# The second channel weight rounded beside the attention and kept in DRAM, and three of the four first token products made of seven smaller products

## The chip, the core and the metric

The program runs on one core of one Trainium2 chip. The core has five engines that run their own instruction streams in order: TensorE (PE in the profile; its weight loads are PEld), VectorE (DVE), ScalarE (ACT), GpSimd (POOL) and SyncE (SP), which here only issues transfers. They hand work to each other by semaphores. The metric is the device time of one execution in microseconds (us); the kernel before has a median of 803.48 us over 5 runs, from 801.98 to 804.40.

## The reference

```python
# attention, 4 batches x 8 heads, S = 768, D = 64; 6 hash bits for each query and key
mask   = q_bucket[:, :, :, None] == k_bucket[:, :, None, :]
scores = scale * np.matmul(q, k.transpose(0, 1, 3, 2))
scores = np.where(mask, scores, -1000000000.0)
attn   = softmax(scores);  x = np.matmul(attn, v)          # (B, S, H*D) = (4, 768, 512)
# mixer: tokens, then channels
h  = np.maximum(x.transpose(0, 2, 1) @ w_tok1, 0.0) @ w_tok2   # 768 -> 256 -> 768
u  = x + h.transpose(0, 2, 1)
h2 = np.maximum(u @ w_ch1, 0.0) @ w_ch2                        # 512 -> 1536 -> 512
out = u + h2
```

The four weights arrive as 64-bit floats. The kernel turns each into 32-bit floats itself ("rounding" below).

## The kernel before

The kernel has three stages after each other, every one with its own pools and with its instructions in the order in which the source writes them: `attention`, `tokens`, `channels`. A fourth part behind a branch is taken only for inputs of large size and does not run here.

**Attention** loops over 16 pairs of heads (n = 0 to 15, four pairs for a batch), and each pair has two halves of 384 queries. For a half, `scores` makes six score tiles: two 32-bit products of keys and queries (L337, `sc<-qk`), then two short bf16 products with the hash bits (L337, `sc<-bits`), which push scores of unequal buckets far down. ScalarE makes the exponential of each tile (L344, `e`), VectorE adds the six tiles up (`add` and `add_last`: L371, L375, L378, tile `esd`), and `weigh` multiplies with the values (L389, `acc`). Three score tiles fit in PSUM; the hash product and one `acc` take their turns in the same ring of three.

The hash bits of pair n+1 are made in pair n by `hashes`: a product (L298, `hp`), VectorE's sign test (L302, `g`), ScalarE's scaling (L303), and eight small transfers by SyncE into the tile `bits` (L308). Transfer 0 to 3 hold what the first half's queries and the first three key blocks need, transfers 6 and 7 the last three key blocks. In the order of pair n's instructions `hashes(n + 1)` stands after the adds of both halves but the last one, then come `add_last`, `load_qk(n + 2)`, `add_values` (L289), rounding, and the normalisation of pair n-1 (`newton` L426 and L428, copies L434, `divide` L438). Behind every second pair, `bounce` transposes two pairs into DRAM (L233, L238), from where `fetch` reads a batch back in token order (L245).

Rounding is the class `Conversion`. A block is 128 x 768 numbers: `fetch` loads its raw words (L169, 768 KB), `begin` is one ScalarE instruction (L177), `join` four VectorE instructions (L187, L191, L195, L196), and `end` one more (L206) that writes the rounded block. `one()` is begin, join, end and the next fetch; `turnover()` is end and fetch. In the attention the blocks of `w_tok1`, `w_tok2` and `w_ch1` (12 in all) are rounded, one in each of pairs 0 to 11, with two buffers of raw words and one fetch ahead. The eight blocks of `w_ch2` are rounded in the stage `tokens`, one by one as "jobs" between its products, straight into the tile `WC2`.

**Tokens** loops over the four batches. `mix1(b)` is the first token product: 12 products with 512 columns (L634), each shown as two rows because a 32-bit product takes two passes; ScalarE applies relu (L641). `mix2(b, m)` is the second token product, already written as seven products in place of eight (L674) with ScalarE copies (L679 to L686), VectorE adds (L689 to L693) and `left_sums` (L657 to L660); its result goes by an accumulating transfer from GpSimd (L694) into `XT`. The results are collected in three `places`, so the transfer of a place has to land before the place is written again. The order is mix1(0), mix1(1), mix2(0,0), mix2(0,1), mix1(2), and so on; at the end come mix2(3,0), mix2(3,1). Both token stages use eight PSUM banks in turn. `weight_sums` of the first channel weight (L724 to L729) is the first job.

**Channels** (L761 and the rows around it) follows with products of the same seven-for-eight kind. Its last one writes four quarters of the output, each with a transfer of its own: L1173, L1180 and twice L1185, issued by ScalarE in the very last product and by SyncE in the one before.

```python
            weights.begin()
            if before:
                before.newton()
            weights.join()
            halves[0].weigh()
            ...
            if before:
                before.divide()
            weights.turnover()
            halves[1].weigh()
```

Of the kernel before, what the change touches and what calls it, by code (L numbers as in the profile page):

```python
# [34 lines left out]
F32 = mybir.dt.float32  # L37
BF16 = mybir.dt.bfloat16
U32 = mybir.dt.uint32
# [9 lines left out]
def kernel(  # L49
# [13 lines left out]
    nc = tc.nc  # L63
# [77 lines left out]
    class Conversion:  # L141


        def __init__(self, pool, parts, bufs):
            self.pool, self.bufs = pool, bufs
            self.todo = [
                (w, dst, rows, j, n)
                for w, dst, rows, blocks in parts
                for j in range(*blocks, rows)
                for n in range(0, dst.shape[2], NW // rows)  # L150
            ]
            self.fetched, self.begun, self.ready = [], None, None
            for _ in range(bufs - 1):
                self.fetch()
# [25 lines left out]
        def join(self):  # L180
            if not self.begun:
                return
            raw, size, to, rows = self.begun
            self.begun = None
            unit = self.pool.tile([P, NW], F32, name="unit", tag="unit", bufs=1)

            nc.vector.tensor_scalar(  # L187
                unit.bitcast(U32), size.bitcast(U32), 3, 0x7F800000,
                op0=ALU.logical_shift_left, op1=ALU.bitwise_and,
            )  # L190
            nc.vector.tensor_scalar(  # L191
                size.bitcast(U32), size.bitcast(U32), 3, None, op0=ALU.logical_shift_left,
            )

            nc.vector.scalar_tensor_tensor(unit, raw[:, :, 0], 2.0**-52, unit, op0=ALU.mult, op1=ALU.mult)  # L195
            nc.vector.tensor_tensor(size, size, unit, op=ALU.add)  # L196
            self.ready = raw, size, to, rows

        def end(self):

            if not self.ready:
                return
            raw, size, to, rows = self.ready
            self.ready = None
            hi, size = (a.rearrange("p (t n) -> p t n", t=rows) for a in (raw[:, :, 1], size.bitcast(U32)))
            nc.vector.scalar_tensor_tensor(  # L206
                to.bitcast(U32), hi, 0x80000000, size, op0=ALU.bitwise_and, op1=ALU.bitwise_or,
            )

        def turnover(self):  # L210
# [13 lines left out]

    dram = ctx.enter_context(tc.tile_pool(name="dram", bufs=1, space=bass.MemoryType.DRAM))
    bounced = [dram.tile([S, DM], F32, name=f"bounced{b}") for b in range(B)]

# [30 lines left out]
    def attention(pool, psum, W1, W2, x0):  # L258
# [191 lines left out]
        for _ in range(12):  # L450
# [3 lines left out]
            pool,  # L454
            [(w_tok1, W1, 3, (0, NR)), (w_tok2, W2, 1, (0, NJ)), (w_ch1, WC1, 1, (0, NCB))],
            bufs=2,
# [4 lines left out]
        for n in range(len(pairs)):  # L461
# [3 lines left out]
            for now in halves:  # L465
                now.scores()
                if n == now.half == 0:
                    hashes(1)
                now.add()
                if now.half == 0:  # L470
                    now.add_last()
            if before:
                before.sums()
# [20 lines left out]
            if before:  # L494
                before.divide()
            weights.turnover()
            halves[1].weigh()
            if n and n % 2 == 0:
# [93 lines left out]

    def tokens(pool, psum, W1, W2, x0, weights, jobs, T, places):

# [5 lines left out]
        R1 = {}  # L600
        turned = not jobs
        if not turned:
            fetch(1, x1)
            jobs = jobs(weights(pool))
            bounce(places[2], len(pairs) - 2)
        NQ = DM // 2
        sums = pool.tile([P, 3, HALF], F32, name="W2sums", tag="W2sums", bufs=1)
        b00, b01, b10, b11 = (W2[:, k, HALF * n : HALF * n + HALF] for k in range(2) for n in range(2))

        def weight_sums():  # L610
            nc.vector.tensor_tensor(sums[:, 0], b01, b00, op=ALU.subtract)
            nc.vector.tensor_tensor(sums[:, 1], b11, sums[:, 0], op=ALU.subtract)
            nc.vector.tensor_tensor(b01, b11, b01, op=ALU.subtract)
            nc.vector.tensor_tensor(sums[:, 2], b10, sums[:, 1], op=ALU.subtract)

        def job():
            if not turned and jobs:
                jobs.pop(0)()

# [3 lines left out]
        def banks():  # L623
            return psum.tile([P, 2, 512], F32, name="trp", tag="tr", bufs=2)

        def mix1(b):
            x = (x0, x1)[b % 2]
            if b and turned:
                turn(b, x, banks)
            r1 = pool.tile([P, NJ, DM], F32, name="r1", tag="r1", bufs=2)  # L630
            for j in range(NJ):
                ps = bank("t1")
                for r in range(NR):
                    nc.tensor.matmul(  # L634
                        ps, W1[:, r, P * j : P * j + P], x[:, r], start=(r == 0), stop=(r == NR - 1),
                    )
                to = r1[:, j]
                if not turned:
                    to = to.rearrange("p (c g i) -> p g c i", c=NCB, i=32)
                    ps = ps.rearrange("p (g c i) -> p g c i", c=NCB, i=32)  # L640
                nc.scalar.activation(to, ps, ACT.Relu)  # L641
                job()
            if b % 2:
# [3 lines left out]
            R1[b] = r1, new  # L647
            if not turned and b + 2 < B:
                fetch(b + 2, x)

# [11 lines left out]
        def mix2(b, m):  # L662
# [5 lines left out]
            new = new[:, :, P * m : P * m + P]  # L668
            ps = [bank("t2")[:, :HALF] for _ in range(4)]
            to = places[(2 * b + m + 1) % 3].rearrange("p (i n t) -> p i n t", i=2, n=2)  # L670
            p1, u, p7, p57 = (to[:, i, n] for i in range(2) for n in range(2))

            def product(at, left, right, start=True):
                nc.tensor.matmul(  # L674
                    ps[at], left, right, start=start, stop=True, skip_group_check=True,
                )

            product(0, a00, b00)
            nc.scalar.copy(p1, ps[0])  # L679
            product(1, a01, b10)  # L680
            product(2, s1, sums[:, 0])
            nc.scalar.copy(p57, ps[2])
            product(3, new[:, 1], b01)
            nc.scalar.copy(p7, ps[3])
            product(0, new[:, 0], sums[:, 1], False)
            nc.scalar.copy(u, ps[0])  # L686
            product(2, new[:, 2], b11, False)
            product(3, a11, sums[:, 2], False)
            nc.vector.tensor_tensor(p1, ps[1], p1, op=ALU.add)  # L689
            nc.vector.tensor_tensor(p57, p7, p57, op=ALU.add)  # L690
            nc.vector.tensor_tensor(p57, p57, u, op=ALU.add)  # L691
            nc.vector.tensor_tensor(p7, ps[3], u, op=ALU.add)
            nc.vector.tensor_tensor(u, ps[2], u, op=ALU.add)  # L693
            nc.gpsimd.dma_start(  # L694
                out=XT[:, 2 * m : 2 * m + 2, S * b : S * b + S], in_=to.rearrange("p i n t -> p i (n t)"),
                accum_op=ALU.add,
            )

        for b in range(B):
            mix1(b)  # L700
            if b == 0:
                weight_sums()
            left_sums(b)
            if b:
                mix2(b - 1, 0)
                job()
                mix2(b - 1, 1)
        mix2(B - 1, 0)
        inputs(0, T, 0)
        mix2(B - 1, 1)  # L710
        while not turned and jobs:
            job()

# [19 lines left out]
    def channels(pool, psum, SW1, second, TA, judge):  # L733
# [399 lines left out]
        def product(s, j, name, q, between, final=None):  # L1133
# [38 lines left out]
            if final:  # L1172
                issuer.dma_start(out=final(0, 0), in_=qs[:, 0])  # L1173
            nc.vector.tensor_tensor(p57[:, 0], p57[:, 0], p57[:, 1], op=ALU.add)
            if j < 6 and final:
                begin(ORDER[j + 1])
            if final:
                nc.vector.tensor_tensor(qs[:, 3], qs[:, 3], u, op=ALU.add)
                nc.vector.tensor_tensor(qs[:, 3], qs[:, 3], p57[:, 0], op=ALU.add)
                issuer.dma_start(out=final(1, 1), in_=qs[:, 3])  # L1180
                for i in (1, 2):
# [177 lines left out]
    def attention_and_tokens(W1, W2, x0):  # L1359
# [12 lines left out]

        def weights(pool):
            return Conversion(pool, [(w_ch2, WC2, 3, (0, NHT))], bufs=3)

        def jobs(conversion):
            early, late = weight_sums(
                WC1, SW1, slice(0, NCB // 2), slice(NCB // 2, NCB), slice(0, DCH // 2), slice(DCH // 2, DCH),
            )
            return [  # L1380
                lambda: (early(), late()),
                *[conversion.one] * (NHT * DM // NW),
            ]

        SW2 = second["SW2"].rearrange("p i k c -> p i (k c)")
        places = [SW2[:, i] for i in range(3)]
        inside(tokens, W1, W2, x0, weights, jobs, [TA[:, 0], None, TA[:, 1], None], places)

    def careful_attention_and_tokens(W1, W2, x0):
# [11 lines left out]
        TA = big["TA"]  # L1401
        with tc.tile_pool(name="places", bufs=1, reuse_waits="tile") as pool:
            places = [pool.tile([P, 2 * S], F32, name=f"place{i}") for i in range(3)]
            inside(tokens, W1, W2, x0, None, None, [TA[:, 0], None, TA[:, 1], None], places)

# [49 lines left out]
```

## Time and profile before

| | |
|---|---|
| median of 5 runs | 803.48 us (801.98 to 804.40) |
| the profiled execution: its own time | 804.27 us |
| the profiled execution: its span | 802.5 us |
| PE busy | 792.8 us, 99% of the span |
| DVE busy | 657.8 us, 82% |
| ACT busy | 441.5 us, 55% |
| attention, from the first product to the first L634 | up to 315.5 us of the span |
| tokens, L634 to the first L761 | 315.5 to 394.0 us |
| channels, L761 | 394.0 to 794.8 us, then the last adds and transfers |

Times in the text are microseconds from the start of the span. A row of the timeline has a start, a length, the engine, the source line, the operation, the tiles (written <- read), the shape and a count of merged instructions; in brackets stands the idle time of that engine just before, with what ended it. A "q" after an engine's name means its sequencer, as when it issues a transfer. The span is 1.77 us shorter than that execution's own time, and that execution is 0.79 us above the median of the runs.

### The profile page before, as it was taken

To read this page: it belongs to the slowest core of one execution; us is meant where nothing else is said; L and a number is where in the kernel's file an instruction comes from. 1 tells how busy PE (TensorE), PEld (TensorE's weight loads), DVE (VectorE), ACT (ScalarE), POOL (GpSimd) and SP (SyncE) were. 2 spreads that over 40 slices of the span, in tenths; PEclk is the share of its full clock that TensorE was granted. 3 is DMA by queue.
4 is the path that set the end of the run, shared out by engine and by line. 5 is a ranking of instruction groups with operands and counts; after the bars stand their busy time and mean duration, and the time that the engine had idled before them with its cause. 6 is when DMAs were issued, how large, how long until landed. Compare 5 with 4: busy or idle time off the path is not lost.

```text
span 802.5 us, 10594 instructions
## 1 busy us (share of the span) xinstructions
PE 792.8 (99%) x3885; PEld 470.7 (59%) x3885; DVE 657.8 (82%) x881; ACT 441.5 (55%) x707; POOL 53.7 (7%) x77
## 2 busy tenths in 40 slices
PE   9999999999999999999999999999999999999996
PEld 5444444444444444455444458876667886666885
DVE  4889898989887677999677888988769897679985
ACT  5688888888888886333222221327782335774110
POOL 1000000000000000011121010011110012100010
PEclk9999999999999999999999999999999999999998
DMA  4435353537352424797636994599754577630455
GB/s 163 159 121 160 121 160 121 161 121 239 126 168 91 148 71 158 199 292 176 155 68 207 312 378 165 179 292 287 212 150 147 208 200 198 208 105 15 175 179 113
DMA packets 90972, 138.61 MB, mean 173 GB/s; under 512 B 29656, under 2 KB 63392, under 8 KB 88608
## 3 DMA queue, kind: packets, MB, share of 16 engines
q1 hardware_dynamic: 82192, 112.20, 42.1%
q0 software_dynamic: 7728, 24.64, 13.7%
q10 hardware_dynamic: 992, 1.00, 0.4%
q8 instruction: 33, 0.54, 0.3%
q14 instruction: 27, 0.22, 0.1%
HBM read 97.21 MB, written 33.16 MB: 162 GB/s over the span
## 4 chain that ended last, share of the span: by engine, by line
PE 95%; DVE 2%; DMA 1%; issue 0%; ACT 0%; DVEq 0%; ACTq 0%
PE b L761 50%; PE sc L337 20%; PE acc L389 16%; PE t L634 4%; PE t L674 2%; PE sums L413 2%; PE hp L298 1%; DMA XT<-second 1%; PE hw L316 1%; PE idle L451 0%; DVE size L196 0%; DVE unit L195 0%; DVE second L693 0%; DVE second L691 0%; DVE second L689 0%
## 5 line engine op out<-in xcount | busy, mean ns | idle before, releaser
L344 ACT ACTIVATE e<-sc 128x768 f32<-128x768 f32 x192 | 154.0, 811 | 12.7 <-PE sc L337 12.3
L337 PE MATMUL sc<-qk 64*128 64x384 f32 x768 | 156.7, 487 | 0.0
L761 PE MATMUL b<-R,second 128*128 128x256 f32 (+1 forms) x612 | 150.9, 404 | 0.0
L761 PEld LDWEIGHTS b<-R,second 128*128 128x128 f32 x612 | 116.3, 190 | 31.6 <-issue 17.2
L767 ACT COPY c<-b 128x512 f32<-128x512 f32 (+1 forms) x78 | 37.5, 488 | 169.1 <-PE b L761 158.5
L389 PE MATMUL acc<-e,vn 128*64 128x384 f32 x768 | 127.6, 488 | 0.0
L375 DVE TENSOR_TENSOR esd<-esd,e 128x768 f32<-128x768 f32 x96 | 92.0, 958 | 10.0
L389 PEld LDWEIGHTS acc<-e,vn 128*64 128x64 f32 x768 | 53.6, 137 | 73.1 <-issue 71.1
L337 PEld LDWEIGHTS sc<-qk 64*128 64x128 f32 x768 | 67.5, 187 | 49.1 <-issue 47.6
L761 PE MATMUL b<-XT,WC 128*128 128x256 f32 (+1 forms) x264 | 82.5, 456 | 0.0
L761 PEld LDWEIGHTS b<-XT,WC 128*128 128x128 f32 x264 | 50.2, 190 | 29.6 <-issue 24.9
L337 PE MATMUL sc<-bits 64*128 64x384 bf16 x384 | 62.9, 323 | 0.2 <-DVE bits L320 0.2
L371 DVE SCALAR_TENSOR_TENSOR esd<-e 128x768 f32<-128x768 f32 x32 | 30.6, 955 | 28.1 <-ACT e L344 28.1
L634 PE MATMUL t<-x,W 128*128 128x512 f32 x96 | 41.8, 593 | 0.0
L694 POOL DMA_DIRECT2D XT<-second x8 | 9.9, 1232 | 392.1 <-DVE second L693 366.1
L395 ACT ACTIVATE num<-acc,vsum 128x384 f32<-128x384 f32 x32 | 18.6, 581 | 31.8 <-PE acc L389 31.4
L434 ACT COPY rec<-rec 32x384 f32<-32x384 f32 x64 | 32.6, 509 | 5.0 <-DVE rec L428 4.2
L761 PE MATMUL b<-XT,SW 128*128 128x256 f32 (+1 forms) x120 | 34.6, 422 | 0.0
L337 PEld LDWEIGHTS <-bits 64*128 64x128 bf16 x384 | 19.3, 94 | 25.4 <-DVE bits L320 0.8
L761 PE MATMUL b<-TA,WC 128*128 128x512 f32 x72 | 33.8, 592 | 0.0
L761 PE MATMUL b<-TA,SW 128*128 128x512 f32 x72 | 32.9, 592 | 0.0
L378 DVE TENSOR_TENSOR esd<-esd,e 128x768 f32<-128x768 f32 x32 | 30.5, 954 | 1.9
(214 smaller groups left out, 1131.1 us busy)
## 6 DMA issues: line engine op xcount, KB each, us to landing
second<-left SPq DMA_DIRECT2D x18, 1344.0 KB
raw<-in_moe_w_ch SPq DMA_DIRECT2D x16, 768.0 KB
qk<-in_qk SPq DMA_DIRECT2D x15, 768.0 KB
seen<-in_qk POOLq DMA_DIRECT2D x21, 384.0 KB, 3.9
WC<-hidden_left SPq DMA_DIRECT2D x15, 448.0 KB
vn<-in_v SPq DMA_DIRECT2D x16, 384.0 KB
vt<-in_vT SPq DMA_DIRECT2D x16, 384.0 KB
x<-bounced SPq DMA_DIRECT2D x4, 1536.0 KB
```

What stands on the lines that cost most here:

```text
L337: nc.tensor.matmul(sc[:, i, :HALF], t[rows, 1, P * c : P * c + P], t[rows, 0, qs], start=start, stop=not start,)
L344: nc.scalar.activation(e, sc[:, :, :HALF], ACT.Exp, scale=SCALE)
L371: nc.vector.scalar_tensor_tensor(self.d, es[0], NR * EPS, es[1], op0=ALU.add, op1=ALU.add,)
L375: nc.vector.tensor_tensor(self.d, self.d, e, op=ALU.add)
L378: nc.vector.tensor_tensor(self.d, self.d, self.es[-1], op=ALU.add)
L389: nc.tensor.matmul(acc[D * i : D * i + D], vn[:, i, c], e[:, i], start=(c == 0), stop=(c == NR - 1),)
L395: nc.scalar.activation(nums[self.n][:, self.half], acc, ACT.Identity, scale=-1.0, bias=vsum,)
L413: nc.tensor.matmul(ps[at : at + 32], ones[:, :32], self.halves[h].d[:, i], start=True, stop=True,)
L434: nc.scalar.copy(rec[other : other + 32, h], rec[at : at + 32, h])
L634: nc.tensor.matmul(ps, W1[:, r, P * j : P * j + P], x[:, r], start=(r == 0), stop=(r == NR - 1),)
L761: nc.tensor.matmul(ps, left(k), right(k), start=start and k == ks[0], stop=stop and k == ks[-1], skip_group_check=True,)
L767: nc.scalar.copy(c, ps)
```

## The change

1. The eight blocks of `w_ch2` join the list that the attention rounds, so there are 20 blocks for 16 pairs. One block is rounded in each pair as before, now in all 16, and in pairs 1, 5, 9 and 13 a second one by `weights.one()`, between the adds of the first half and those of the second half. One more fetch at the end of pair 0 puts the raw words two blocks ahead. A rounded block of `w_ch2` is written to the tile `unit` and from there by a SyncE transfer to a DRAM tile `wc2`; after mix1(0) one transfer brings all 3 MB of it into `WC2`. The conversions in `tokens` are gone.
2. mix1(1), mix1(2) and mix1(3) are made of seven products each, three instructions of 256 columns to a product, with sums of `W1` made once (`left`, four VectorE instructions), sums of x for every such batch (`right_sums`, four), four ScalarE copies and five VectorE adds (`seven`, which mix2 now shares), and two relus afterwards (`relus`). mix1(0) keeps its full product, in 24 instructions of 256 columns in place of 12 of 512. The two halves of the sums of the first channel weight are jobs after batches 0 and 1.
3. In the last channel product the first two of the four output transfers are issued by SyncE, the last two by ScalarE as before.

```diff
             away = to.space == bass.MemoryType.DRAM
             nc.vector.scalar_tensor_tensor(
-                to.bitcast(U32), hi, 0x80000000, size, op0=ALU.bitwise_and, op1=ALU.bitwise_or,
+                (unit if away else to).bitcast(U32), hi, 0x80000000, size,
+                op0=ALU.bitwise_and, op1=ALU.bitwise_or,
             )
+            if away:
+                nc.sync.dma_start(out=to, in_=unit)
...
-            [(w_tok1, W1, 3, (0, NR)), (w_tok2, W2, 1, (0, NJ)), (w_ch1, WC1, 1, (0, NCB))],
+            [
+                (w_tok1, W1, 3, (0, NR)), (w_tok2, W2, 1, (0, NJ)), (w_ch1, WC1, 1, (0, NCB)),
+                (w_ch2, wc2, 3, (0, NHT)),
+            ],
             bufs=2,
...
                 now.add()
                 if now.half == 0:
                     now.add_last()
+                    if n % 4 == 1:
+                        weights.one()
...
             weights.turnover()
+            if n == 0:
+                weights.fetch()
             halves[1].weigh()
...
+        def right_sums(b):
+            x00, x01, x10, x11 = quarters(b)
+            nc.vector.tensor_tensor(right[:, 0], x01, x00, op=ALU.subtract)
+            nc.vector.tensor_tensor(right[:, 1], x11, right[:, 0], op=ALU.subtract)
+            nc.vector.tensor_tensor(x01, x11, x01, op=ALU.subtract)
+            nc.vector.tensor_tensor(right[:, 2], x10, right[:, 1], op=ALU.subtract)
...
+            seven([bank("t1")[:, :NQ] for _ in range(4)], to, [
+                (u00, x00), (u01, x10), (s1, t1), (s3, x01), (s2, t2), (s4, x11), (u11, t4),
+            ])
...
+        weight_sums()
+        if not turned:
+            bounce(places[2], len(pairs) - 2)
+            right_sums(1)
         for b in range(B):
+            if b and turned:
+                turn(b, (x0, x1)[b % 2], banks)
+                right_sums(b)
             mix1(b)
-            if b == 0:
-                weight_sums()
+            if not turned:
+                if b + 2 < B:
+                    fetch(b + 2, (x0, x1)[b % 2])
+                if b == 0:
+                    nc.sync.dma_start(out=second["WC2"], in_=wc2)
+                elif b + 1 < B:
+                    right_sums(b + 1)
+            if b:
+                mix2(b - 1, 0)
+                relus(b)
             left_sums(b)
             if b:
-                mix2(b - 1, 0)
-                job()
                 mix2(b - 1, 1)
+            if jobs:
+                jobs.pop(0)()
...
             if final:
-                issuer.dma_start(out=final(0, 0), in_=qs[:, 0])
+                nc.sync.dma_start(out=final(0, 0), in_=qs[:, 0])
...
-                issuer.dma_start(out=final(1, 1), in_=qs[:, 3])
+                nc.sync.dma_start(out=final(1, 1), in_=qs[:, 3])
```

## The prediction

> **What bounds the kernel now.** I read the page first, then the chain of waits, then the timeline of one pair of the attention, the transfers in a small window, and the timelines of the token stage and of the end.
>
> ```profile
> PE 792.8 (99%) x3885; PEld 470.7 (59%) x3885; DVE 657.8 (82%) x881; ACT 441.5 (55%) x707; POOL 53.7 (7%) x77
> ```
>
> ```profile
> by line: PE b L761 49.9%; PE sc L337 19.7%; PE acc L389 15.8%; PE t L634 3.9%; PE t L674 2.4%; PE sums L413 1.6%; PE hp L298 1.2%; DMA XT<-second 1.2%; PE hw L316 0.5%; PE idle L451 0.4%; issue 0.3%; DVE size L196 0.2%; DVE unit L195 0.2%;
> ```
>
> TensorE is the bound everywhere. The chain shows each pair of the attention at the same 19.21 us of products without a gap. So an edit gains only what it takes from TensorE, and costs only where it makes TensorE wait. The question is how near the others are to making it wait. Pair 3 (from 65.5) into pair 4 (from 84.72):
>
> ```profile
> 67.88 0.36 PEld L337 LDWEIGHTS sc<-qk 64*128 64x128 f32 x4 [0.22 <-issue]
> 68.28 0.96 DVE L371 SCALAR_TENSOR_TENSOR esd<-e 128x768 f32<-128x768 f32 x1 [0.62 <-ACT e L344]
> 73.41 0.95 DVE L371 SCALAR_TENSOR_TENSOR esd<-e 128x768 f32<-128x768 f32 x1
> 74.47 3.08 DVE L375 TENSOR_TENSOR esd<-esd,e 128x768 f32<-128x768 f32 x3
> 77.47 0.55 DVE L302 TENSOR_SCALAR g<-hp 128x384 bf16<-128x384 f32 x1
> 78.05 0.61 ACT L303 ACTIVATE g<-g,bitscale 128x384 bf16<-128x384 bf16 x1 [0.68 <-DVE g L302]
> 78.69 5.90 SPq L308 DMA_DIRECT2D bits<-g  x8
> 84.84 0.58 ACT L395 ACTIVATE num<-acc,vsum 128x384 f32<-128x384 f32 x1 [1.82 <-PE acc L389]
> 87.49 0.96 DVE L371 SCALAR_TENSOR_TENSOR esd<-e 128x768 f32<-128x768 f32 x1 [2.38 <-ACT e L344]
> 87.58 0.10 PEld L337 LDWEIGHTS <-bits 64*128 64x128 bf16 x2
> 87.90 0.33 PE L337 MATMUL sc<-bits 64*128 64x384 bf16 x2
> ```
>
> VectorE has no idle time from 68.28 to the sign test at 77.47, which begins as soon as the adds let it. ScalarE and then SyncE follow at once. The bandwidth row of the window from 78 to 90 us (slices of 0.3 us) shows the eight bit transfers as eight small bursts:
>
> ```profile
> GB/s 0 0 0 0 0 0 5 13 0 18 0 5 13 0 18 0 15 3 0 18 0 18 0 0 18 164 61 143 328 369 410 410 430 369 471 369 389 430 410 338
> ```
>
> The first burst is at about 80.1 to 80.2, so 1.5 us after its issue at 78.69; issues are 5.90 / 8 = 0.74 apart, so the eighth is at 85.3 to 85.4 (slice 25, 85.2 to 85.5). It is first needed by the fourth score tile of pair 4: its load is at 87.58, its product at 87.90, a load lasts 0.10, so it may come at 87.80. Less 0.06 for the signal, the slack is 87.80 - 85.36 - 0.06 = 2.4 us.
>
> **Part 1, twenty blocks in the attention.** The price of a block on VectorE is in the token stage, where blocks follow each other:
>
> ```profile
> 327.57 0.56 DVE L187 TENSOR_SCALAR unit<-size 128x768 uint32<-128x768 uint32 x1
> 330.61 0.96 DVE L206 SCALAR_TENSOR_TENSOR second<-raw,size 128x768 uint32<-128x768 uint32 x1
> 331.49 0.55 DVE L611 TENSOR_TENSOR W2sums<-W 128x384 f32<-128x384 f32 x1
> ```
>
> 331.49 - 327.57 = 3.92 us. In pairs 12 to 15 the added block stands where pairs 0 to 11 have it without a gap on TensorE: no cost. In pairs 1, 5, 9 and 13 the second block stands ahead of the second half's adds, so of the sign test too, on an engine without idle time: the test, ScalarE's scaling behind it and the eight transfers all come 3.92 later. Of that 2.4 is slack; 3.92 - 2.38 = 1.54 us of waiting at the fourth tile (about 1 us of it already at the first, whose four transfers have more slack). Two other chains give no more. On ScalarE the block's first instruction (0.92 long, 0.83 to the next start) stands between exponentials: a score tile's buffer is free again after an exponential that ends 0.41 ahead of its next use (first exponential 66.66 + 0.81 = 67.47, load 67.88), so TensorE waits about 0.83 - 0.41 = 0.4, which is part of the 1.54 and not on top. Behind the late scaling ScalarE runs L289, L177, L434 and two L395 without a gap (4.3 us), and starts the next exponentials 1.5 late: the same size. On VectorE 3.92 less the 2.38 idle at 87.49 is again 1.5. So the pair after begins in step, and four times 1.54 is **+6.2 us**. Bounds: 0.4 a time, +1.7, if only the ScalarE instruction shows; 3.9 a time, +15.7, if nothing covers. The two end rows of that slack are of this very loop, so I take 6.2.
>
> The Trainium skill has a rule against adding to this chain: the page "DMA: Bandwidth & Descriptors", in its anatomy of one DMA, gives a fixed cost of about 2.0 us for a transfer (a fit on the GpSimd path), mostly completion. The row says 1.5. By the page's figure, as an estimate, the bits would land 0.5 later and the sum be 2 us higher.
>
> Raw words (768 KB at the 410 GB/s of the row: 1.9 us) are fetched just after the block's end, 5 us ahead of the late bits, so they are through by then. Stores of a block (384 KB) and 3 MB back into `WC2` run under products; `WC2` is first read in the channel stage. Without that cover the load would cost 3.1 / 0.41 = 7.7 us. In pair 15 VectorE has 4.5 us idle, in which the block fits; the last store makes SyncE wait to about 317, and x of batch 1, fetched at 306.0 before, is issued behind it. Its 1.5 MB (3.8 us and 1.5 to begin) land at about 324, needed at 326.
>
> **Part 2, the token stage.**
>
> ```profile
> 345.26 10.46 PE L634 MATMUL t<-x,W 128*128 128x512 f32 x24
> 489.38 1.46 PE L761 MATMUL b<-second,second 128*128 128x256 f32 x6
> 391.99 0.91 PE L674 MATMUL t<-W2sums,r1s 128*128 128x384 f32 x2 [0.82 <-ACT second L679]
> ```
>
> Twenty-four rows last 10.30 us to the next start (0.43 each); six rows of 256 columns take 1.30 (0.216). Seven products of three instructions are 42 rows, 9.06 us: 1.24 less, three times, **-3.7**. Batch 0 becomes 48 x 0.216 = 10.35, no change. VectorE loses eight blocks (31 us) and gains 4 W1 sums (2), three right_sums (3.75 each), three times five adds (2.1 each): less work. Batch 1's sums stand behind W1 and W2 sums and the transposes: from the last division (it ends at 318.7, with pair 15's block some 0.6 later) 319.3 + 4.0 + 1.8 + 3.75 = 328.9; its third product, first to need one, begins at 325.95 + 2.6 = 328.5 and needs the first sum (326.1). Later batches have more room. If VectorE did come late, each microsecond would show, as no product is left to run ahead. The gap of 0.82 at 391.99 came from a place's transfer that took 9.8 us to land (median of these rows 6.8). With less queued on VectorE its adds end about 0.5 earlier against the products, so the gap is 0.3 at 9.8 us and none at 6.8: **-0.7**, between 0 and -0.8. Part 2 together -4.4.
>
> **Part 3, the end.**
>
> ```profile
> 794.23 1.91 ACTq L1180 DMA_DIRECT2D out<-second  x1
> 796.23 1.13 ACTq L1185 DMA_DIRECT2D out<-second  x2
> ```
>
> ScalarE's second issue lasts 1.91 and holds back the last two, whose adds end at 795.2 and 795.6. With SyncE taking the first two, they go 0.8 to 1.0 earlier: **-0.8**, between 0 (the same transfer engines are what is slow) and -1.3.
>
> **Sum.** 6.2 - 4.4 - 0.8 = +1.0 us. On the profiled execution, 804.27, that is 805.3; this execution was 0.79 above the median, so the median becomes 803.48 + 1.0 = **804.5 us**. A measurement of this kernel can tell about 0.2%, 1.6 us, from no change, so the likeliest verdict is no change, on the slow side. Own range of this case: 802.8 to 806.2 (attention 5 to 7.5, tokens -3.7 to -4.5, end 0 to -1.3).
>
> **The rivals.**
>
> *The bits come later still (slower).* Place: the eight transfers of pairs 1, 5, 9, 13 queue behind the second raw fetch, which now sits between them and idle transfer engines. It decides if those raw words are not through when the bits are issued, at 82.6 in the frame above; up to 1.9 us more, four times, +7.6: up to 812. Against it: 5 us between the two issues. For it: nothing in this trace puts big transfers ahead of bits in odd pairs. Half of that price, +3.8, is 808.3.
>
> *The delay is covered (faster).* If the bits had 1.2 us more room than my reading of the bursts, only ScalarE's 0.4 is left: 1.7 - 4.4 - 0.8 = -3.5, 800.0. Against it: the continuous VectorE rows; for it: the window view is coarse, 0.3 us a slice.
>
> *x of batch 1 comes late (slower).* It is now issued 11 us later, with 2 us of room. Each microsecond beyond 326 is a microsecond: with 1 to 4, 805.5 to 808.5. For it: 256-byte stores and the block's store share the engines then.
>
> **How the numbers follow.** Sum as forecast 0.42; later bits 0.27; covered delay 0.18; late x 0.13. Faster by over 0.2% comes from the covered delay (0.18) and a sliver of the first: 0.19. Within: 0.32 of the first, 0.02 and 0.06 of the slow ones: 0.40. Slower: 0.09, 0.25, 0.07: 0.41. The range 801.0 to 808.5 leaves out about half of the covered case and the upper part of the later bits, some 0.2.
>
> **What would show it.** Right: gaps on TensorE of 1.0 to 1.2 in all at the first and fourth score tiles of pairs 2, 6, 10 and 14, released by bit transfers, and 0.4 inside pairs 1, 5, 9 and 13, released by `e`; the sign test 3.9 later there; each seven-product mix1 at 9.06; no gap before the last mix2; ScalarE's last issue before 796.6. Wrong: no such gaps in the attention, gaps in ordinary pairs, or a gap at the first product of mix1(1).

## The result, and the profile after

The changed kernel takes 805.37 us (median of 37 runs, 803.62 to 806.98), the kernel before 803.46 us (62 runs, 801.54 to 806.66). The ratio is 1.0025, with a 95% interval from 1.0019 to 1.0031: 1.9 us slower. The profiled execution of after took 805.29 us, with a span of 803.5.

First the page's busy line, then two of its groups, the products with the hash bits and their weight loads (busy, mean of one in ns, then the idle time ahead of them and what ended it), and last the first of these groups in the page of before:

```profile
PE 792.8 (99%) x3963; PEld 490.1 (61%) x3963; DVE 674.8 (84%) x912; ACT 442.9 (55%) x721; POOL 53.3 (7%) x77
L348 PE MATMUL sc<-bits 64*128 64x384 bf16 x384 | 67.8, 323 | 3.2 <-DMA bits<-g 2.7
L348 PEld LDWEIGHTS <-bits 64*128 64x128 bf16 x384 | 22.4, 94 | 30.7 <-DMA bits<-g 8.7
L337 PE MATMUL sc<-bits 64*128 64x384 bf16 x384 | 62.9, 323 | 0.2 <-DVE bits L320 0.2
```

TensorE is as busy in all as before (792.8), although products were taken away. A hash product is as long as it was (323 ns), but the group is busy for 67.8 us in place of 62.9. A tile has two of these products, one for each head, which otherwise run beside each other; where the bits of the two heads land one after the other, the products run one after the other too, and the busy time grows. So only part of the waiting shows as idle time ahead of the group (3.2 us, 0.2 in before). The releaser names where: `bits<-g`, the eight small transfers. The chain that ended last, in order of time, leaves TensorE at the first such place, from pair 1 into pair 2 (some of its pieces):

```profile
42.96 0.48 DVE g L313
43.46 0.62 ACT g L314
44.10 0.74 SPq L319
46.37 2.15 DMA bits<-g
48.57 9.34 PE sc L348 x67
```

In before no step of an ordinary pair's chain was anything but TensorE. Here it runs over VectorE (the last adds of the first half, the added block, the adds of the second half), ScalarE, SyncE's issues and a transfer. The timeline from pair 5 (from 105.58) into pair 6 (from 125.05) shows it engine by engine:

```profile
113.11 0.30 PEld L348 LDWEIGHTS sc<-qk 64*128 64x128 f32 x4 [0.54 <-ACT e L355]
116.51 0.96 DVE L213 SCALAR_TENSOR_TENSOR WC<-raw,size 128x768 uint32<-128x768 uint32 x1
117.39 0.95 DVE L382 SCALAR_TENSOR_TENSOR esd<-e 128x768 f32<-128x768 f32 x1
121.45 0.55 DVE L313 TENSOR_SCALAR g<-hp 128x384 bf16<-128x384 f32 x1
122.68 5.90 SPq L319 DMA_DIRECT2D bits<-g  x8
126.04 0.33 PE L348 MATMUL sc<-bits 64*128 64x384 bf16 x1
126.78 0.33 PE L348 MATMUL sc<-bits 64*128 64x384 bf16 x1 [0.41 <-DMA bits<-g]
129.71 0.33 PE L348 MATMUL sc<-bits 64*128 64x384 bf16 x1 [0.24 <-DMA bits<-g]
```

The score tile behind `size` waits for an exponential (0.54 where 0.22 is usual). The block ends at 117.4, the second half's adds begin only then, the sign test comes at 121.45 (3.60 ahead of the next pair; in an ordinary pair 7.26), and TensorE waits for the bits at its first and its fourth tile.

Read off the starts of the pairs, and of the stages behind them, the profiled executions compare so:

| us | before | after |
|---|---|---|
| to the start of pair 1 | 27.10 | 27.00 |
| pairs 1, 5, 9, 13 | 19.21 each | 19.46 to 19.48 |
| pairs 2, 6, 10, 14 | 19.21 each | 20.70 to 20.72 |
| pairs 3, 4, 7, 8, 11, 12 | 19.21 each | 19.21 each |
| pair 15 | 19.50 | 19.50 |
| pair 1 to the first token product | 288.43 | 295.44 |
| tokens | 78.51 | 73.78 |
| channels | 400.76 | 400.76 |
| last product to the end of the span | 7.69 | 6.51 |

So the attention lost 7.01 us, the tokens gained 4.73. (Channels are counted to the end of the last product.) The token stage in TensorE's timeline:

```profile
322.44 10.63 PE L707 MATMUL t<-x,W 128*128 128x256 f32 x48
332.91 1.89 PE L662 MATMUL t<-x,W 128*128 128x256 f32 x8
395.58 0.81 PE L662 MATMUL t<-W2sums,r 128*128 128x384 f32 x2
396.22 1.02 PE L843 MATMUL b<-XT,WC 128*128 128x512 f32 x2
```

The seven products of batch 1 follow the full product of batch 0 at once, so neither x of batch 1 nor its sums are late, and no gap is left to the end of the stage.

### The profile page after: what moved, and what is told of

Same layout as the page of the kernel before. It is cut to its first block, busy times and chain, and to the rows that moved or that the text cites. A ratio compares the mean times of both kernels' runs of the same rounds, so it can differ in the third digit from the quotient of the medians.

```text
span 803.5 us, 10811 instructions
## 1 busy us (share of the span) xinstructions
PE 792.8 (99%) x3963; PEld 490.1 (61%) x3963; DVE 674.8 (84%) x912; ACT 442.9 (55%) x721; POOL 53.3 (7%) x77
## 4 chain that ended last, share of the span: by engine, by line
PE 87%; DVE 4%; SPq 3%; ACT 2%; DMA 2%; issue 1%; DVEq 0%
PE b L843 50%; PE sc L348 14%; PE acc L400 11%; PE t L662 8%; SPq L319 2%; ACT e L355 2%; PE t L707 1%; DVE esd L386 1%; PE sums L424 1%; DMA vt<-in_vT 1%; DMA bits<-g 1%; PE hp L309 1%; SPq L249 1%; PE hw L327 0%; DMA raw<-in_moe_w_ch 0%
## 5 line engine op out<-in xcount | busy, mean ns | idle before, releaser
L355 ACT ACTIVATE e<-sc 128x768 f32<-128x768 f32 x192 | 151.9, 812 | 12.3 <-PE sc L348 12.0
L348 PE MATMUL sc<-qk 64*128 64x384 f32 x768 | 158.4, 489 | 0.0
L348 PEld LDWEIGHTS sc<-qk 64*128 64x128 f32 x768 | 69.5, 187 | 46.4 <-issue 40.0
L348 PE MATMUL sc<-bits 64*128 64x384 bf16 x384 | 67.8, 323 | 3.2 <-DMA bits<-g 2.7
L348 PEld LDWEIGHTS <-bits 64*128 64x128 bf16 x384 | 22.4, 94 | 30.7 <-DMA bits<-g 8.7
L843 PEld LDWEIGHTS b<-XT,SW 128*128 128x128 f32 x120 | 22.8, 190 | 10.8 <-issue 7.0
```

The lines of the kernel that those rows point to most:

```text
L348: nc.tensor.matmul(sc[:, i, :HALF], t[rows, 1, P * c : P * c + P], t[rows, 0, qs], start=start, stop=not start,)
L355: nc.scalar.activation(e, sc[:, :, :HALF], ACT.Exp, scale=SCALE)
L843: nc.tensor.matmul(ps, left(k), right(k), start=start and k == ks[0], stop=stop and k == ks[-1], skip_group_check=True,)
```

## The experiments

The theory on the attention: the block in the middle delays the sign test, and TensorE waits for what exceeds the slack of the bits. Its rivals: the extra load as such, wherever it stands; the raw words' transfers; the ring of score tiles behind ScalarE's instruction. For the rest: whether the tokens' gain is the products', and whether the end's gain is real.

**The block at the end of the pair** (`block_last`).

```diff
-                    if n % 4 == 1:
-                        weights.one()
...
             halves[1].weigh()
+            if n % 4 == 1:
+                weights.one()
```

In pair 13 the first block is stored from another free tile, so that the second need not wait for that store.

> The second block of pairs 1, 5, 9 and 13 is moved from the middle of the pair to its end. Theory (the block delays the sign test, the bits land after their slack): the block now uses VectorE's idle 2.38 us ahead of the next pair's first add and delays the next sign test by only 3.92 - 2.38 = 1.5 us, less than the slack of some 2.2, so no wait for bits is left. First token product at 315.5 to 316.5 instead of 322.5, time 798.5 to 800. Rival 1 (the load of the extra blocks itself costs, wherever they stand): 322, 805. Rival 2 (the raw words' transfers are in the way of the bits): gaps of about 1 us stay in pairs 2, 6, 10 and 14, 802 to 804.

801.07 us (12 runs) against 803.45, ratio 0.997 (0.9956 to 0.9983). Pairs 1, 2, 5, 6, 9, 10, 13, 14 all last 19.21, but pairs 3, 7 and 11 last 19.70 to 19.72 and pair 15 lasts 20.85: 291.29 in all, 4.15 less than after. The same 20 blocks cost 2.9 instead of 7.0, so the load as such is not the price. But the expected zero was missed. VectorE's and ScalarE's rows at the end of pair 1:

```profile
47.73 0.89 ACT L182 ACTIVATE size<-raw 128x768 f32<-128x768 f32 x1
48.65 0.56 DVE L192 TENSOR_SCALAR unit<-size 128x768 uint32<-128x768 uint32 x1 [1.13 <-ACT size L182]
```

ScalarE's instruction stands behind `num`, which waits for the second half's products until 47.25, and its tile is held by the block before until 47.5. So it begins at 47.73, VectorE stands idle for 1.13 of its 2.38 us, and the sign test of pair 2 comes 1.54 + 1.13 = 2.67 late. That is 0.5 more than a slack of 2.17, and 0.5 is what pair 3 lost.

Pair 15 lost 1.35 (19.50 to 20.85). Its sign test is 2.68 late, so 0.5 of this is the same wait. Most of the rest is at its end, where two waits stand that before does not have, both ended by VectorE's normalisation, which now comes too late:

```profile
313.89 0.85 PE L427 MATMUL sums<-esd,ones 128*32 128x384 f32 x8 [0.25 <-DVE t L440]
319.21 10.63 PE L712 MATMUL t<-x,W 128*128 128x256 f32 x48 [0.45 <-DVE t L440]
```

**The last key blocks' bits first** (`keys_first`).

```diff
-            for j in range(4):
+            for j in (0, 1, 3, 2):
```

> The block stays in the middle; the eight transfers of the bits go out in another order, the four for the first tile, then the two for the last three key blocks, then the two for the second half's queries. Theory: of the 1.4 us that TensorE waits in pairs 2, 6, 10 and 14 about 0.9 is at the first tile and 0.5 at the fourth; the fourth's goes, since its two transfers are issued 1.4 us earlier, and the second half's queries still land in time. First token product at about 320.5, time about 803.4. Rival (not the bits but the ring of score tiles or ScalarE sets that delay): no change, 322.5 and 805.4.

804.41 us (12 runs) against 803.45, ratio 1.0015 (1.0001 to 1.0029). Pairs 6, 10 and 14 last 20.18 to 20.20 in place of 20.70 (pair 2: 20.56), and 293.76 in all. The start of pair 6 (from 125.52):

```profile
127.25 0.33 PE L348 MATMUL sc<-bits 64*128 64x384 bf16 x1 [0.41 <-DMA bits<-g]
129.61 0.39 PE L348 MATMUL sc<-bits 64*128 64x384 bf16 x2
```

The wait at the first tile has stayed, the one at the fourth has gone: 0.50 to 0.52 us of the 1.49, by the order of the transfers alone. It is their landing that TensorE waits for. Four times 0.5 had been expected, and only 1.68 in all came. In pair 2 the wait at the first tile is 0.76 instead of 0.41, since the transfer that ends it lands 2.14 us after its issue there and 1.77 in pair 6, and only 0.14 was gained. Why it lands later in pair 2 wasn't looked for; after shows the same (2.15, in the chain above).

**The four blocks left out** (`left_out`): the middle `one()` is taken away and the list ends with the first four blocks of `w_ch2`.

> The four second blocks are not rounded at all (rows 768 to 1535 of the second channel weight are a copy of rows 0 to 767), all else as after, with as much loaded into WC2. Theory: the whole cost in the attention is theirs; first token product at 315.5, tokens and end as after, 798.4. Rival (raw words two ahead, the stores or the extra block of pairs 12 to 15 cost something too): above 316.5, 800 or more.

798.98 us (4 runs), ratio 0.9946 (0.9925 to 0.9966). All of pairs 1 to 14 last 19.21; 288.43 us from pair 1 to the first token product, as in before. Raw words two ahead, the stores and the blocks of pairs 12 to 15 cost nothing; the 7.01 is the four middle blocks' alone. (The first token product came at 316.9, since pair 1 began at 28.49 here.)

**Their parts, one by one** (`scalar_only`, `vector_only`, `vector_2`, `vector_3`): in that kernel, in place of the middle `one()`, only the ScalarE instruction; only five VectorE instructions of the block's forms; only two, or three, additions:

```diff
+                    if n % 4 == 1:
+                        unit = pool.tile([P, NW], F32, name="unit", tag="unit", bufs=1)
+                        d = now.d.rearrange("p i q -> p (i q)")
+                        for _ in range(2):
+                            nc.vector.tensor_tensor(unit, d, d, op=ALU.add)
```

> As the kernel with the four second blocks left out (288.4 us from the start of the second pair to the first token product), but with the block's ScalarE instruction alone in the middle of pairs 1, 5, 9 and 13 (the same rows of the second channel weight are copies). Each theory of the wait: those four pairs last 19.48 instead of 19.21 (one exponential later by 0.83, less the ring's slack), and pairs 2, 6, 10 and 14 last 19.21. 289.5 in all. Rival (a late exponential throws the pair after out of step too): 19.5 and more in both.

> As the kernel with the four blocks left out, but with five VectorE instructions of the block's forms and sizes (3.92 us) in the middle of pairs 1, 5, 9 and 13, and no ScalarE instruction, raw fetch or store there. Theory 1 (one delay: 3.92 less a slack of 2.17, and ScalarE's 0.27 is part of it): those pairs 19.21, the pairs after them 19.21 + 1.75 = 20.96, 295.4 in all. Theory 2 (ScalarE's 0.27 comes on top of the late bits): 19.21 and 20.70, 294.4. Rival (the raw words' fetch in the middle makes the bits late): the pairs after last below 20.3.

> As the kernel with the four blocks left out, but with two additions of 128 x 768 on VectorE (2 x 0.96 = 1.9 us) in the middle of pairs 1, 5, 9 and 13. Theory (a slack of about 2.2 before TensorE waits): all pairs 19.21. Rival (VectorE has no idle time there, so each microsecond shows in part): pairs 2, 6, 10 and 14 above 19.4.

> The same with three additions, 2.9 us. By a slack of 2.38, as predicted: pairs 2, 6, 10 and 14 last 19.21 + 0.5 = 19.7. By a slack of 2.17, as the kernel after suggests: 19.9 to 20.0, 3 us in all. Rival (a wait in proportion to the delay, 1.75 for 3.92): 20.5.

One execution each: 800.05, 807.16, 798.80 and 802.97 us. ScalarE's instruction alone lengthens its own pairs to 19.46 or 19.47 and leaves the next at 19.21: the ring is worth 0.26, no more. The VectorE kernels leave their own pairs at 19.21. For the pairs behind, the start of the sign test, compared with the usual 7.26 us ahead of the next pair, against the lengthening of that pair:

| kernel, pair | sign test late by | pair longer by | difference |
|---|---|---|---|
| two additions, 2, 6 and 14 | 1.99 | 0 | |
| two additions, 10 | 2.34 | 0.15 | 2.19 |
| block at the pair's end, 3 | 2.67 | 0.50 | 2.17 |
| three additions, 2 and 6 | 2.98 | 0.80 | 2.18 |
| three additions, 14 | 3.34 | 1.15 | 2.19 |
| after, 6 | 3.66 | 1.49 | 2.17 |
| five instructions, 10 | 4.18 | 2.00 | 2.18 |
| five instructions, 6 | 4.53 | 2.34 | 2.19 |

One line through all of these: nothing up to 2.18 us, then microsecond for microsecond. A wait in proportion to the delay is out, and so is a separate part for the raw fetch, which the VectorE kernels don't have in the middle. The five instructions delayed the sign test by 4.18 us, not by the 3.92 that I had counted; so this kernel missed both of its numbers (20.96 and 20.70), and only the line decides between its theories. In after VectorE is 3.92 later on the clock, but its pair has become 0.26 longer by then: 3.66 late against the products. The two waits together are 0.26 + 1.49 = 1.75 = 3.92 - 2.17. ScalarE's wait is part of the delay and does not come on top. (Pair 2 of `vector_only` lasted 23.01; see the last section.)

**The full product in place of the seven** (`plain_mix1`): mix1(1) to mix1(3) made like mix1(0), without `right_sums` and `relus`.

> The first token product of batches 1 to 3 is the full one again, 48 rows of 256 columns, without its sums; all else as after. Theory (products are what counts): 6 rows of 0.216 more for each of three batches, tokens 73.8 + 3.7 = 77.6 us long (1.24 each is 48 x 0.216 less 42 x 0.216), time 809. Rival (the gain came from VectorE's lighter queue, not from the products): tokens below 75.5, time below 807.

809.07 us (4 runs), ratio 1.0076 (1.0055 to 1.0097). Tokens last 77.67: 3.89 more than after, and 0.84 less than before. So 3.89 of the 4.73 is the products', and 0.84 is what the rest of part 2 gives, the size of the gap of 0.82 that stood ahead of the last mix2 and is gone.

**The end** (`end_only`: before with part 3 alone; `end_back`: after with part 3 undone).

```diff
-                issuer.dma_start(out=final(0, 0), in_=qs[:, 0])
+                nc.sync.dma_start(out=final(0, 0), in_=qs[:, 0])
...
-                issuer.dma_start(out=final(1, 1), in_=qs[:, 3])
+                nc.sync.dma_start(out=final(1, 1), in_=qs[:, 3])
```

> The kernel before with the third part of the change alone (the first two of the last four output transfers issued by SyncE). Theory 1 (the prediction's 0.8, and the 1.2 between the two profiled executions): 802.3 to 802.7. Theory 2 (the profiled execution of before had an end that was long by chance; the sums of the other runs leave 0.2 to 0.4 for this part): 803.1 to 803.4. The last product to the end of the span: 5.9 to 6.5 us in both.

> The kernel after with the third part undone (all four of the last transfers issued by ScalarE). Theory 1: 7.7 us from the last product to the end of the span, as in the profiled execution of before. Theory 2: some execution of this order ends sooner, 6.3 to 7.

Part 3 alone gives 803.01 us (12 runs) against 803.16, ratio 1.000 (0.999 to 1.001). That lies between the two expectations; no gain is shown, and the interval leaves room for up to 0.8 us either way. With it undone in after, the end of the span comes 5.85 us after the last product, sooner than with it (6.51). ScalarE's issues with it undone:

```profile
796.76 0.66 ACTq L1262 DMA_DIRECT2D out<-second  x1
797.82 0.91 ACTq L1267 DMA_DIRECT2D out<-second  x2
```

The second issue takes 0.66 here and took 1.91 in the profiled execution of before. In `end_only` SyncE's took 1.32. So the length of this issue varies between executions in both orders. From the last product to the end of the span it takes 7.69 and 5.85 us in the two traces without part 3 and 5.02 to 6.78 in the eleven with it: the ranges overlap. What makes an issue long wasn't tried.

**A version without the wait** (`best`): the second blocks at the end of pairs 1, 3, 7 and 11, bits in the order of `keys_first`, and ScalarE's instruction into a free half of the tile `stage`, ahead of the second half's products.

```diff
+            second_block = n in (1, 3, 7, 11)
...
             weights.turnover()
...
+            if second_block:
+                weights.begin(stage[:, NW:])
             halves[1].weigh()
+            if second_block:
+                weights.join()
+                weights.turnover()
```

> The second blocks go to the end of pairs 1, 3, 7 and 11, with the ScalarE instruction ahead of the second half's products (into a tile that is free there) so that VectorE's idle 2.38 us are used whole, and the bits in the order that serves the key blocks first. Theory: the sign test is late by 1.5 us (2.4 after pair 3, where little idle time was left), the slack is 2.18 + 0.5 in this order, so no wait in the attention: 288.4 to 288.8 us from the second pair to the first token product (after: 295.4), time 798.5 to 799.5. Rival (ScalarE's instruction now delays the first exponentials): up to 0.4 in each of four pairs, 290, 800.5.

798.73 us (6 runs) against 803.16, ratio 0.9943 (0.9931 to 0.9956): faster than both kernels. Pairs 1 to 14 all last 19.21, and 288.43 in all. VectorE at the end of pair 1 (from the last instruction of the first block to the next pair's first add; rows between them are left out):

```profile
46.17 0.95 DVE L217 SCALAR_TENSOR_TENSOR W<-raw,size 128x768 uint32<-128x768 uint32 x1
47.04 0.56 DVE L193 TENSOR_SCALAR unit<-stage 128x768 uint32<-128x768 uint32 x1
50.96 0.95 DVE L386 SCALAR_TENSOR_TENSOR esd<-e 128x768 f32<-128x768 f32 x1
```

The two blocks and the next first add follow without idle time. The sign test is then 1.5 late, and 2.2 after pair 3; neither makes TensorE wait. (The slack is larger in this order of the bits: in `keys_first` the sign test is 3.67 late and pair 6 loses 0.99, so some 2.7.)

## Why the prediction was right or wrong

**The verdict and the mechanism: right.** 804.5 was forecast, 805.37 measured, inside the range and on the slow side. The slowdown itself, 1.9 us, is a little above the 1.6 that was called no change; the prediction called no change likeliest, though its own chances put "slower" (0.41) level with it (0.40). The waits are where they were said to be: at the first and fourth tiles of pairs 2, 6, 10 and 14, released by the bits (1.49 a pair, where 1.0 to 1.2 was said), and behind `size` (0.26, where 0.4 was said).

**Attention, +6.2: mis-sized by 0.8.** The term that was too large is the slack, 2.38 against a measured 2.18. The prediction took 1.46 us from issue to the burst in the bandwidth row, and 0.06 for the signal. The chain of after shows the eighth transfer of pair 5:

```profile
127.89 1.77 DMA bits<-g
129.66 0.05 issue
129.71 6.79 PE sc L348 x49
```

That is 1.77 + 0.05 = 1.82 from its issue to TensorE, 0.3 more than the 1.52 counted. The signal was right; the bandwidth row shows when the bytes move, and the transfer counts as landed 0.3 later. On the other side, 0.10 was kept free for the weight load, while here load and product both start at 129.71. The two leave the 0.2 by which the slack was too large. The Trainium skill, in the page "DMA: Bandwidth & Descriptors", anatomy of one DMA, gives about 2.0 us for the whole way, mostly completion. For the whole way its figure was nearer than mine, though its price for the sum, 2 us more, was above the 0.8 that came. That most of it is completion does not show here: of 1.77 us only 0.3 lie behind the bytes. And what the page states is this cost, not a rule against adding to such a chain. That ScalarE's part is contained and not added held.

**Tokens, -4.4: right.** -4.73 measured; the products gave 3.89 where 3.7 was counted, the gap 0.84 where 0.7 was.

**The end, -0.8: this step failed.** No gain of it was found (0.15 us between medians, within the noise). The prediction took one issue of 1.91 us, seen once, as the price of the order; in another execution of that order the issue takes 0.66, and ScalarE's last two issues begin as soon after the last product as with part 3 (0.5 us in both). Without this term the sum is 6.2 - 4.4 = +1.8; with the measured terms +7.0 - 4.7 = +2.3. The medians differ by 1.9, so up to some 0.4 may still be the end's, or noise. The two profiled spans differ by only 1.0, because the end of before's span is 1.2 longer: 7.0 - 4.7 - 0.1 - 1.2. That this equals the forecast's +1.0 is luck: against the forecast the attention is off by +0.8, the tokens by -0.3, and start and end together by -0.5.

**The rivals.** Later bits, behind the raw fetch: `vector_only` lies on the same line without that fetch, so no. A covered delay would have needed 1.2 us more slack; there were 0.2 less. Late x of batch 1: no gap stands there.

## What to carry to other kernels

When work is added to an engine that is not the bound, ask what stands behind it in that engine's queue and how long the path from there to the bound may be late: the price is the delay less that slack, nothing at all below it. Place it behind the last producer that the bound waits for, where the engine has idle time, and make sure its inputs and its tiles are free by then: the same four blocks cost 7.0 us in the middle of a pair, 2.9 at its end with ScalarE's part too late, and 0 with that part ahead (there partly in other pairs, and with the bits reordered). A single slow issue at the end of one trace is no term of a sum until a second execution shows it.

## What the runs showed of the hardware

A wait can cost more than itself; this was seen once. In pair 2 of `vector_only` TensorE waited twice in a row for bits (0.59 and 1.01 us idle), and the stretches of 1 us show what followed (the busy time of PE, PEld, DVE, ACT and POOL, then the granted clock, the DMA share and GB/s):

```profile
47.00:48.00 1.00, 0.41 (x5) 0.02 (x1) 1.00 (x2) 0.98 (x3) 0.00 (x0) 1.00 0.02 5
48.00:49.00 1.00, 0.32 (x1) 0.07 (x1) 0.97 (x2) 0.97 (x3) 0.00 (x0) 1.00 0.05 17
49.00:50.00 1.00, 0.67 (x5) 0.56 (x7) 1.00 (x2) 0.73 (x2) 0.00 (x0) 0.92 0.03 8
50.00:51.00 1.00, 1.00 (x7) 0.69 (x4) 1.00 (x2) 0.51 (x1) 0.00 (x0) 0.50 0.02 5
51.00:52.00 1.00, 1.00 (x5) 0.47 (x4) 0.20 (x2) 0.81 (x1) 0.00 (x0) 0.50 0.40 67
52.00:53.00 1.00, 1.00 (x7) 0.83 (x5) 0.80 (x1) 0.40 (x1) 0.00 (x0) 0.50 0.82 276
53.00:54.00 1.00, 1.00 (x10) 0.70 (x8) 0.56 (x1) 0.60 (x2) 0.00 (x0) 0.88 0.98 412
```

The clock is granted at 0.92 in 49 to 50, 0.50 for three stretches, 0.88 in the last: 1.70 us lost, that is 3.4 us at half speed, and the pair was 3.80 longer where pairs 10 and 14, equally late, were 2.0 longer. The Trainium skill, in the page "TensorE: Matmul & The Clock Gate", Part 1, puts the gate's window at about 3.4 us, which agrees; it says that an idle window throttles, while here TensorE was busy for 1.4 of the 3 us from 47 to 50. In the later pairs of this run, which lost 2.0 to 2.3 us, and in the other profiled runs, whose pairs lost up to 1.5, the clock stayed at full speed. What made the difference isn't shown.

The start and the end of the span differ between executions although their code is alike: pair 1 began between 26.98 and 28.67, and the last product was 5.02 to 7.69 from the end. The stretch between repeats: from pair 1 to the first token product it is 295.44, 295.40 and 295.44 us in the three traces with the same attention (after, `plain_mix1`, `end_back`). So a part of that stretch is better measured by the starts of its pairs in one trace than by medians of the whole.
